# A fused attention and gated MLP kernel: four scalings and eight small copies given to GpSimd instead of ScalarE

## The chip, the cores and the metric

The kernel runs on one core of a Trainium2 chip, as one launch. The metric is the device time of that launch in microseconds (us), the median of several runs; lower is better. The core has TensorE (PE in the profile, PEld its weight loads), VectorE (DVE), ScalarE (ACT), GpSimd (POOL) and SyncE (SP), which here issues the DMAs.

## What is computed

Attention with a near window and pooled far keys, and behind it a gated MLP:

```python
# q, k, v: (4, 8, 768, 64); window 16, pooling block 32
k_sum = k.reshape(B, H, nb, block, D).max(axis=3)
v_sum = v.reshape(B, H, nb, block, D).mean(axis=3)
scores = concat([where(|i-j| < window, scale * q @ k.T, -1e9),
                 scale * q @ k_sum.T + log(block)], axis=-1)
a = exp(scores - max);  a = a / (sum(a) + 1e-9)
x = a @ concat([v, v_sum])          # -> (3072 tokens, 512)
g = x @ w_gate                      # (512, 1536)
out = (g * sigmoid(g) * (x @ w_val)) @ w_out
```

The weights arrive as 64-bit floats. The kernel turns them into float32 with integer arithmetic on DVE.

## The kernel before

The 3072 tokens are worked in 6 blocks of 512. Within a block, attention goes by 4 pairs of heads (u = 0 to 3, 128 channels each) and the MLP by 12 slices of the hidden size (j = 0 to 11). To keep precision, each MLP operand is split into a high and a low part, so that every product is three matmuls: the gate (g), the value (v) and the down projection (acc) of a slice are 12 matmuls of 128x512 each.

Two things run beside the MLP of block 0, from about 60 to 142 us. One is the attention of block 1. The other is the making of the weights: per tile `w_load` (DMA), `w_abs` (ACT, L212), `w_c1` and `w_c2` (DVE, one input, L217 and L221), `w_s1` and `w_s2` (DVE, two inputs, L229 and L236), `w_hi` (a rounding copy, mostly ACT, L187) and `w_lo` (a subtraction, DVE or POOL, L183). "gv" is a slice's gate and value weights (1024 columns), "o" its down weights (512).

The order of this stage is written out by hand in a table, PROLOGUE. Each word is a step with its arguments, and a letter behind "=" names the engine (a ScalarE, d VectorE, p GpSimd). Every engine runs its instructions strictly in the order of the table. From block 1 on, a loop sets the order.

Block 1's attention for pair u has these steps: `load`, `keys(1,u)` (pooled keys beside the near keys, POOL copies, L189), `scores` (PE, L434), `ttr0/1` (bias and row maximum, DVE, L481), `exp0/1` (ACT, L496), `rcp` (1e-9 added, reciprocal, DVE, L513 and L514), `nrm` (probabilities p times the reciprocal ri), `tr0/1` (transposes on PE, L537), `pt0/1` (copies out of PSUM, ACT), `values(1,u)` (pooled values into the rows behind the near values vw), `out` (PE, L584), `split` and `rest` (high and low part for the MLP). Block 1 spans two batch entries, so `values(1,u)` is four parts: a copy of the old pooled rows `vs` (24x512), a transpose on PE (pv, L370), a scaling of its result by 1/32 from PSUM into `vs` by ACT (L371), and a second copy. The second copy reads what L371 wrote, and L371 overwrites what the first copy read. There is one buffer of vw. The MLP's `ah` and `al` are the high and low part of the hidden activations (L187 and L183); `al(0,j)=p` is a subtraction on POOL that `down(0,j)` needs first.

The two functions that read the engine's letter (variable `on`):

```python
def a_scale(k, u):
    p, ri = U[k, u]["p"], U[k, u]["ri"]
    if on == "a":
        for i in range(2 * NTP):
            nc.scalar.mul(p[:, i, :], p[:, i, :], ri[:, i : i + 1])   # L520
        return
    (nc.vector if on == "d" else nc.gpsimd).tensor_tensor(            # L522
        out=p, in0=p, in1=ri.rearrange(...).broadcast_to([P, 2 * NTP, p.shape[2]]), op=ALU.mult)

def a_values(k, u):   # for each batch entry of the block
    nc.scalar.mul(vsum["all"][...], pv[:NB, :P], 1.0 / BLK)           # L371, if the entry begins here
    copy(on or "d", U[k, u]["vw"][KW:, i : i + n], pooled(u).broadcast_to([NB, n, P]))
```

Of the kernel before, what the change touches and what calls it, by code (L numbers as in the profile page):

```python
# [122 lines left out]
w_s1(4,gv) w_c1(3,o) w_s2(4,gv) exp1(1,0) w_hi(1,o)=a w_c2(3,o) w_lo(1,o)=d exp0(1,0) w_hi(4,gv)=a w_s1(3,o)  # L123
w_c2(2,o) w_s2(3,o) w_s1(2,o) w_load(7,gv) w_load(6,gv) rcp(1,0) down(0,1) w_lo(4,gv)=d load(1,1) silu(0,3)
w_abs(5,gv) w_hi(3,o)=a w_c1(5,gv) mul(0,3) gate(0,4) val(0,4) ah(0,2)=a w_abs(7,gv) w_c2(5,gv) w_lo(3,o)=d
w_s1(5,gv) w_s2(2,o) nrm(1,0)=a w_hi(2,o)=a w_s2(5,gv) al(0,2)=d w_hi(5,gv)=a tr0(1,0) silu(0,4) w_abs(6,gv)
w_load(4,o) tr1(1,0) pt0(1,0)=a w_abs(4,o) w_lo(2,o)=d pt1(1,0)=a down(0,2) keys(1,1) mul(0,4) w_c1(6,gv)
w_lo(5,gv)=d w_c1(4,o) scores(1,1) ah(0,4)=a w_c2(6,gv) ah(0,3)=a ttr0(1,1) exp0(1,1) ttr1(1,1) al(0,4)=d
w_load(5,o) load_values(1,0) w_load(7,o) w_load(6,o) w_c1(7,gv) w_s1(6,gv) values(1,0)=a w_load(9,gv) gate(0,5)
al(0,3)=p w_abs(5,o) w_c2(4,o) w_s2(6,gv) w_load(8,gv) w_s1(4,o) val(0,5) w_c2(7,gv) w_hi(6,gv)=a down(0,3)  # L130
out(1,0) silu(0,5) w_lo(6,gv)=d w_s2(4,o) w_c1(5,o) w_s1(7,gv) gate(0,6) w_abs(6,o) mul(0,5) w_hi(4,o)=a
w_lo(4,o)=p down(0,4) pool_values(1,1) w_s2(7,gv) w_c2(5,o) load_values(1,1) exp1(1,1) w_c1(6,o) w_s1(5,o)
w_abs(7,o) w_abs(9,gv) w_c1(9,gv) w_c1(7,o) val(0,6) w_hi(7,gv)=a w_lo(7,gv)=d w_c2(9,gv) split(1,0)=a w_s2(5,o)
rcp(1,1) silu(0,6) w_abs(8,gv) w_c2(6,o) w_s1(9,gv) load(1,2) mul(0,6) rest(1,0) w_hi(5,o)=a w_c2(7,o) ah(0,5)=a
values(1,1)=a al(0,5)=p w_load(8,o) w_load(10,gv) w_s1(6,o) gate(0,7) silu(0,7) nrm(1,1)=a w_load(9,o) val(0,7)
w_c1(8,gv) w_lo(5,o)=d w_s2(9,gv) w_hi(9,gv)=a tr0(1,1) down(0,5) mul(0,7) ah(0,7)=a pt0(1,1)=a keys(1,2)
scores(1,2) pool_values(1,2) tr1(1,1) w_lo(9,gv)=d w_s2(6,o) w_abs(8,o) w_s1(7,o) gate(0,9) ttr0(1,2) ttr1(1,2)
pt1(1,1)=a w_c2(8,gv) out(1,1) ah(0,6)=a load(1,3) w_hi(6,o)=a w_lo(6,o)=d exp0(1,2) al(0,6)=p w_s2(7,o)
w_c1(8,o) exp1(1,2) w_hi(7,o)=a w_s1(8,gv) al(0,7)=d w_s2(8,gv) w_c2(8,o) val(0,9) down(0,6) w_lo(7,o)=d
w_abs(10,gv) w_abs(9,o) w_c1(9,o) w_hi(8,gv)=a w_c1(10,gv) w_lo(8,gv)=d down(0,7) silu(0,9) rcp(1,2) w_c2(10,gv)  # L140
w_s1(10,gv) mul(0,9) split(1,1)=a w_s2(10,gv) w_c2(9,o) nrm(1,2)=a gate(0,8) tr0(1,2) w_hi(10,gv)=a keys(1,3)
w_lo(10,gv)=d w_s1(8,o) val(0,8) ah(0,9)=a rest(1,1) room(1) w_load(11,v) w_load(11,g) silu(0,8) mul(0,8)
load_values(1,2) w_load(10,o) w_load(11,o) w_s2(8,o) pt0(1,2)=a al(0,9)=p w_abs(11,v) ah(0,8)=a w_hi(8,o)=a
w_s1(9,o) al(0,8)=d w_lo(8,o)=d gate(0,10) w_c1(11,v) tr1(1,2) pt1(1,2)=a w_c2(11,v) w_s2(9,o) w_s1(11,v)
w_s2(11,v) scores(1,3) ttr0(1,3) values(1,2)=a w_hi(9,o)=a silu(0,10) down(0,8) ttr1(1,3) val(0,10) w_abs(11,g)
w_c1(11,g) w_c2(11,g) w_lo(9,o)=p out(1,2) w_s1(11,g) w_s2(11,g) w_abs(10,o) exp1(1,3) w_hi(11,g)=d w_c1(10,o)
w_hi(11,v)=a down(0,9) w_lo(11,g)=p exp0(1,3) split(1,2)=d mul(0,10) w_lo(11,v)=d w_c2(10,o) rcp(1,3) ah(0,10)=a
rest(1,2) gate(0,11) w_abs(11,o) w_c1(11,o) w_c2(11,o) load_values(1,3) nrm(1,3)=a w_s1(10,o) tr0(1,3)
pt0(1,3)=a w_s2(10,o) al(0,10)=d w_hi(10,o)=a silu(0,11) pool_values(1,3) val(0,11) tr1(1,3) pt1(1,3)=a
values(1,3)=a w_s1(11,o) w_lo(10,o)=d down(0,10) w_s2(11,o) out(1,3) w_hi(11,o)=d w_lo(11,o)=p mul(0,11)  # L150
ah(0,11)=d al(0,11)=d split(1,3)=a down(0,11) rest(1,3) load(2,0)
"""

# [730 lines left out]
```

## Time and profile before

| | |
|---|---|
| median of 3 runs (lowest to highest) | 678.55 us (678.51 to 678.67) |
| the profiled execution | 678.02 us |
| its span in the profile | 676.2 us |
| PE busy | 670.1 us (99% of the span) |
| PEld busy | 543.5 us (80%) |
| DVE busy | 331.3 us (49%) |
| ACT busy | 298.1 us (44%) |
| POOL busy | 134.4 us (20%) |

The busy shares are averages over a first part that is crowded on DVE and ACT (attention and weight making beside the MLP) and a long second part where they are half idle. What counts for a change in the first part is which engine's work PE meets late there. A busy PE is a sum of modelled durations: a stall of a few tenths between two matmuls hides in it.

### The profile page before, as it was taken

Reading aid. Unit: us, or ns where it says so; the run is one execution under the profiler, and the core shown is the slowest. Engines: PE = TensorE matmul, PEld = TensorE weight load, DVE = VectorE, ACT = ScalarE, POOL = GpSimd, SP = SyncE. Lnnn points to the kernel's source line nnn. Section 1 sums busy time; section 2 is a strip of 40 time slices with the busy share of each in tenths; the row PEclk is TensorE's granted clock in tenths of the full one; section 3 lists DMA queues with packets and bytes.
Section 4 is the critical chain, followed back from the end, with each engine's and each line's share of the span. In section 5 each row is a group of like instructions: output and inputs, shape, how many; then the busy total and the mean of one; then the engine's idle time right before and its main releaser. Section 6 shows DMA issues by size and latency. Waiting matters only on the chain.

```text
span 676.2 us, 12388 instructions
## 1 busy us (share of the span) xinstructions
PE 670.1 (99%) x4940; PEld 543.5 (80%) x4940; DVE 331.3 (49%) x919; ACT 298.1 (44%) x729; POOL 134.4 (20%) x130
## 2 busy tenths in 40 slices
PE   8999999999999999999999999999999999999997
PEld 5688888888888888888888888888888888888886
DVE  6999999946624525435346345343352451100011
ACT  6968998844441433424415424235244151211112
POOL 3110112112221212212112122121212121111110
PEclk9999999999999999999999999999999999999999
DMA  8899165145320223302404312012122000100001
GB/s 328 340 373 354 49 234 171 46 120 157 79 58 0 56 48 95 82 24 55 105 24 143 80 49 58 18 38 64 56 57 57 0 25 0 63 1 0 1 0 63
DMA packets 72058, 60.36 MB, mean 89 GB/s; under 512 B 42144, under 2 KB 60064, under 8 KB 70464
## 3 DMA queue, kind: packets, MB, share of 16 engines
q1 hardware_dynamic: 72000, 59.57, 28.6%
q8 instruction: 39, 0.64, 0.4%
q14 instruction: 19, 0.16, 0.1%
HBM read 53.26 MB, written 6.29 MB: 88 GB/s over the span
## 4 chain that ended last, share of the span: by engine, by line
PE 97%; DVE 2%; DMA 1%; issue 0%; SPq 0%; ACT 0%; DVEq 0%; ACTq 0%
PE g L619 30%; PE acc L669 29%; PE v L619 29%; PE xo L584 4%; PE sc L423 2%; DMA kq<-in_kF 1%; PE pp L537 1%; DVE p L481 1%; PE sc L434 1%; PE xo L592 1%; DVE ks L336 0%; PE pv L391 0%; PE pp L693 0%; PE pv L370 0%; DVE m_g L221 0%
## 5 line engine op out<-in xcount | busy, mean ns | idle before, releaser
L669 PE MATMUL acc<-w_o,ah 128*128 128x512 f32 x576 | 177.7, 390 | 0.0
L619 PE MATMUL g<-xh,w_gv 128*128 128x512 f32 x480 | 160.3, 395 | 0.0
L619 PE MATMUL v<-xh,w_gv 128*128 128x512 f32 x480 | 158.0, 390 | 0.0
L183 POOL TENSOR_TENSOR al<-a,ah 128x512 fp32r<-128x512 f32 x63 | 81.7, 1296 | 333.4 <-ACT ah L187 333.4
L630 DVE TENSOR_TENSOR a<-v,a 128x512 f32<-128x512 f32 x72 | 49.7, 690 | 191.6 <-PE v L619 190.8
L669 PEld LDWEIGHTS acc<-w_o,ah 128*128 128x128 f32 x576 | 108.1, 188 | 22.7
L187 ACT CAST ah<-a 128x512 fp32r<-128x512 f32 x71 | 44.0, 621 | 156.8 <-DVE a L630 156.8
L669 PE MATMUL acc<-w_o,al 128*128 128x512 f32 x288 | 113.0, 392 | 0.0
L619 PEld LDWEIGHTS g<-xh,w_gv 128*128 128x128 f32 x480 | 90.1, 188 | 21.1 <-ACT w_o L187 0.2
L619 PEld LDWEIGHTS v<-xh,w_gv 128*128 128x128 f32 x480 | 90.1, 188 | 19.1 <-issue 0.3
L625 ACT ACTIVATE a<-g 128x512 f32<-128x512 f32 x72 | 43.0, 597 | 137.9 <-PE g L619 136.3
L565 DVE STREAM_TRANSPOSE pt_short<-p_short 32x256 f32<-32x256 f32 x192 | 83.8, 436 | 25.9 <-POOL p_short L522 23.2
L619 PE MATMUL g<-xl,w_gv 128*128 128x512 f32 x240 | 93.5, 390 | 0.0
L619 PE MATMUL v<-xl,w_gv 128*128 128x512 f32 x240 | 93.4, 389 | 0.0
L669 PEld LDWEIGHTS acc<-w_o,al 128*128 128x128 f32 x288 | 54.1, 188 | 11.5 <-issue 0.2
L619 PEld LDWEIGHTS v<-xl,w_gv 128*128 128x128 f32 x240 | 45.1, 188 | 9.3
L619 PEld LDWEIGHTS g<-xl,w_gv 128*128 128x128 f32 x240 | 45.1, 188 | 8.8
L496 ACT ACTIVATE p_short<-p_short,nm 128x88 f32<-128x88 f32 x128 | 45.3, 355 | 0.2
L522 POOL TENSOR_TENSOR p_short<-p_short,ri 128x704 f32<-128x704 f32 x16 | 21.8, 1364 | 57.5 <-DVE ri L514 53.6
L619 PE MATMUL g<-xh,w_g 128*128 128x512 f32 x96 | 32.6, 400 | 0.0
L619 PE MATMUL v<-xh,w_v 128*128 128x512 f32 x96 | 31.9, 393 | 0.0
L187 ACT CAST xh<-xo 128x512 fp32r<-128x512 f32 x23 | 13.4, 591 | 38.2 <-PE xo L584 38.2
(108 smaller groups left out, 690.9 us busy)
## 6 DMA issues: line engine op xcount, KB each, us to landing
raw_gv<-in_wgv SPq DMA_DIRECT2D x10, 1024.0 KB, 11.8
raw_o<-in_wo SPq DMA_DIRECT2D x12, 512.0 KB, 7.4
out<-o SPq DMA_DIRECT2D x23, 256.0 KB, 2.0
kt<-in_kP SPq DMA_DIRECT2D x12, 384.0 KB, 4.1
vt<-in_vT SPq DMA_DIRECT2D x12, 384.0 KB, 3.9
vw<-in_vP SPq DMA_DIRECT2D x12, 384.0 KB, 3.8
kw<-in_kP SPq DMA_DIRECT2D x12, 272.0 KB, 4.7
vw<-in_vP SPq DMA_DIRECT2D x16, 192.0 KB, 3.4
```

The costliest lines, as they stand in the source:

```text
L183: (nc.vector if e == "d" else nc.gpsimd).tensor_tensor(out=out, in0=a, in1=b.bitcast(F32), op=ALU.subtract)
L187: nc.scalar.copy(out, in_)
L423: nc.tensor.matmul(sc[h][s * SQ : (s + 1) * SQ, c * SC : (c + 1) * SC], t["q"][hs, i * SQ : (i + 1) * SQ], keys[hs], start=True, stop=True,)
L434: nc.tensor.matmul(sc[h][s * QT : (s + 1) * QT, c * KC : (c + 1) * KC], t["q"][hs, qs], t["kw"][hs, i, :], start=True, stop=True,)
L496: nc.scalar.activation(out=t["p"][:, i, :kc], in_=t["p"][:, i, :kc], func=AF.Exp, scale=-1.0, bias=t["nm"][:, i : i + 1], accum_out=t["sm" ...
L522: (nc.vector if on == "d" else nc.gpsimd).tensor_tensor(out=p, in0=p, in1=ri.rearrange("p (n o) -> p n o", o=1).broadcast_to([P, 2 * NTP, ...
L565: nc.vector.transpose(out=to[r * SQ : (r + 1) * SQ, :, s * SQ : (s + 1) * SQ], in_=t["p"][s * SQ : (s + 1) * SQ, :, at : at + SQ],)
L584: nc.tensor.matmul(ps[hs, qs], vw, t["pt"][:n, h, qs], start=k not in OWN or i == 0, stop=k not in OWN)
L619: nc.tensor.matmul(ps, w[:, cs], x, start=u == 0 and n == 0, stop=u == NP - 1 and n == 2)
L625: nc.scalar.activation(out=a, in_=A.pop(("g", k, j)), func=AF.Silu)
L630: nc.vector.tensor_tensor(out=a, in0=ps, in1=a, op=ALU.mult)
L669: nc.tensor.matmul(ACC[k][i], a[:, ts], w, start=j == 0 and n == 0, stop=j == NJ - 1 and n == 2)
```

## The change

In the table, for block 1 and all four pairs, `nrm(1,u)=a` becomes `nrm(1,u)=p` and `values(1,u)=a` becomes `values(1,u)=p`. No step changes its place.

```diff
-w_s1(5,gv) w_s2(2,o) nrm(1,0)=a w_hi(2,o)=a w_s2(5,gv) al(0,2)=d w_hi(5,gv)=a tr0(1,0) silu(0,4) w_abs(6,gv)
+w_s1(5,gv) w_s2(2,o) nrm(1,0)=p w_hi(2,o)=a w_s2(5,gv) al(0,2)=d w_hi(5,gv)=a tr0(1,0) silu(0,4) w_abs(6,gv)
...
-w_load(5,o) load_values(1,0) w_load(7,o) w_load(6,o) w_c1(7,gv) w_s1(6,gv) values(1,0)=a w_load(9,gv) gate(0,5)
+w_load(5,o) load_values(1,0) w_load(7,o) w_load(6,o) w_c1(7,gv) w_s1(6,gv) values(1,0)=p w_load(9,gv) gate(0,5)
 al(0,3)=p w_abs(5,o) w_c2(4,o) w_s2(6,gv) w_load(8,gv) w_s1(4,o) val(0,5) w_c2(7,gv) w_hi(6,gv)=a down(0,3)
...
```

The same two letters change for pairs 1, 2 and 3. Each scaling, 8 instructions of 128x120 on ACT, becomes one of 128x960 on POOL.

POOL's rows from the weights of slice 3 to the keys of pair 2, before (the number behind a name's last "_" only tells buffers apart; kw_1 and vw_0 are the tiles of pairs 1 and 0, al_3 that of slice 3):

```order
L183 TENSOR_TENSOR w_gv_776<-m_gv_615,w_gv_776 128x1024
L189 COPY kw_1_876<-ks_224 128x4x24
L189 COPY kw_1_876<-ks_973 128x4x24
L183 TENSOR_TENSOR al_3_1052<-a_3_881,ah_3_1001 128x512
L183 TENSOR_TENSOR w_o_1128<-m_o_956,w_o_1128 128x512
L183 TENSOR_TENSOR al_5_1213<-a_5_1106,ah_5_1206 128x512
L189 COPY kw_2_1196<-ks_134 128x4x24
```

The same stretch with the change:

```order
L183 TENSOR_TENSOR w_gv_776<-m_gv_615,w_gv_776 128x1024
L522 TENSOR_TENSOR p_0_780<-p_0_780,ri_0_783 128x960
L189 COPY kw_1_876<-ks_224 128x4x24
L189 COPY kw_1_876<-ks_966 128x4x24
L189 COPY vw_0_1016<-vs_106 24x512 x2
L183 TENSOR_TENSOR al_3_1045<-a_3_881,ah_3_994 128x512
L183 TENSOR_TENSOR w_o_1121<-m_o_949,w_o_1121 128x512
L189 COPY vw_1_1140<-vs_106 24x512 x2
L183 TENSOR_TENSOR al_5_1206<-a_5_1099,ah_5_1199 128x512
L522 TENSOR_TENSOR p_1_996<-p_1_996,ri_1_999 128x960
L189 COPY kw_2_1189<-ks_134 128x4x24
```

Both copies of vw now stand ahead of al_3 and of al_5 on POOL, and the scaling of pair 1 stands behind al_5.

ACT's rows around the pooled values of pair 0, before:

```order
L187 CAST ah_3_1001<-a_3_881 128x512
L496 ACT_TABLE_LOAD
L496 ACTIVATE p_1_1003,sm_1_1005<-p_1_1003,nm_1_1004 128x120 x4
L187 COPY vw_0_1023<-vs_106 24x512
L371 ACTIVATE vs_106<-pv_0_1033 24x128
L187 COPY vw_0_1023<-vs_106 24x512
L212 ACTIVATE m_o_1054<-raw_o_1021 128x512
```

The same stretch with the change:

```order
L187 CAST ah_3_994<-a_3_881 128x512
L496 ACT_TABLE_LOAD
L496 ACTIVATE p_1_996,sm_1_998<-p_1_996,nm_1_997 128x120 x4
L371 ACTIVATE vs_106<-pv_0_1026 24x128
L212 ACTIVATE m_o_1047<-raw_o_1014 128x512
```

The two copies leave ACT; L371 stays there, behind the four exponentials of pair 1. The rows of PE, DVE and SP keep their order.

## Rows read from the trace of the kernel before

**Rows 1.** The page: shares of the chain that ended last, by engine.

```profile
PE 97%; DVE 2%; DMA 1%; issue 0%; SPq 0%; ACT 0%; DVEq 0%; ACTq 0%
```

**Rows 2.** Busy us (instructions) by stretch: PE, PEld, DVE, ACT, POOL; then clock, DMA, GB/s.

```profile
59.60:85.00 25.40, 25.40 (x171) 20.55 (x171) 25.38 (x50) 23.95 (x50) 2.97 (x3) 1.00 0.44 158
85.00:117.50 32.50, 32.50 (x205) 26.49 (x204) 32.01 (x62) 30.04 (x64) 6.26 (x7) 1.00 0.65 202
```

**Rows 3.** Waits, 50 to 152 us: total us, times, longest us.

```profile
DVE m_gv L217 <- ACT m_gv L212: 0.4, 1, 0.4
```

**Rows 4.** Instructions on tiles p and vw: min/median/max ns, first and last start.

```profile
L520 ACT ACTIVATE p<-p,ri x32: 379/384/407, 62.4 to 133.7; 128x120 f32<-128x120 f32 x32
L522 POOL TENSOR_TENSOR p<-p,ri x3: 1790/1791/1847, 11.8 to 17.9; 128x960 f32<-128x960 f32 x3
...
L187 ACT COPY vw<-vs x8: 614/618/619, 74.8 to 139.5; 24x512 f32<-24x512 f32 x8
```

**Rows 5.** Groups by form, POOL's copies of 384 elements: busy us, mean ns.

```profile
L189 POOL COPY kw<-ks 128x384 f32<-128x384 f32 x12 | 6.6, 553 | 18.5 <-PE sc L423 18.5
```

**Rows 6.** Timeline of POOL and DVE: start us, us, operation; pairs that meet.

```profile
14.51 1.85 POOL L522 TENSOR_TENSOR p<-p,ri 128x960 f32<-128x960 f32 x1 [0.88 <-DVE ri L514]
15.49 1.15 DVE L221 TENSOR_SCALAR m_g<-m_g 128x512 int32<-128x512 int32 x1
...
16.68 0.70 DVE L229 SCALAR_TENSOR_TENSOR m_g<-raw_g,m_g 128x512 int32<-128x512 int32 x1
...
17.87 1.79 POOL L522 TENSOR_TENSOR p<-p,ri 128x960 f32<-128x960 f32 x1 [1.51 <-DVE ri L514]
19.22 0.99 DVE L236 SCALAR_TENSOR_TENSOR m_g<-raw_g,m_g 128x512 int32<-128x512 int32 x1
...
83.93 0.41 DVE L221 TENSOR_SCALAR m_o<-m_o 128x512 int32<-128x512 int32 x1
...
115.10 1.22 DVE L183 TENSOR_TENSOR w_gv<-m_gv,w_gv 128x1024 fp32r<-128x1024 f32 x1
115.19 1.26 POOL L189 COPY kw<-ks 128x96 f32<-128x96 f32 x1 [12.50 <-DVE ks L336]
```

**Rows 7.** Timeline of DVE and PE around the scaling of pair 0.

```profile
59.66 1.17 DVE L183 TENSOR_TENSOR w_gv<-m_gv,w_gv 128x1024 fp32r<-128x1024 f32 x1
60.76 0.69 DVE L217 TENSOR_SCALAR m_gv<-m_gv 128x1024 f32<-128x1024 f32 x1
...
66.64 0.68 DVE L183 TENSOR_TENSOR w_o<-m_o,w_o 128x512 fp32r<-128x512 f32 x1
...
67.63 0.63 PE L669 MATMUL acc<-w_o,ah 128*128 128x512 f32 x2
```

**Rows 8.** Timeline of POOL, ACT and PE around the copies of pair 0.

```profile
71.43 1.29 POOL L183 TENSOR_TENSOR al<-a,ah 128x512 fp32r<-128x512 f32 x1 [2.92 <-ACT ah L187]
...
75.43 0.27 ACT L371 ACTIVATE vs<-pv 24x128 f32<-24x128 f32 x1
...
76.82 0.39 PE L669 MATMUL acc<-w_o,al 128*128 128x512 f32 x1
```

**Rows 9.** Timeline of ACT, DVE and PE around pair 1.

```profile
91.70 0.26 ACT L371 ACTIVATE vs<-pv 24x128 f32<-24x128 f32 x1
...
92.60 0.74 DVE L229 SCALAR_TENSOR_TENSOR m_o<-raw_o,m_o 128x512 int32<-128x512 int32 x1
...
94.58 0.60 PE L537 MATMUL pp<-consts,p 128*120 128x128 f32 x4
...
97.93 1.21 DVE L183 TENSOR_TENSOR w_gv<-m_gv,w_gv 128x1024 fp32r<-128x1024 f32 x1
...
99.24 0.48 PE L619 MATMUL g<-xh,w_gv 128*128 128x512 f32 x1
```

**Rows 10.** Timeline of DVE and PE around the scaling of pair 2.

```profile
110.97 1.23 DVE L229 SCALAR_TENSOR_TENSOR m_gv<-raw_gv,m_gv 128x1024 int32<-128x1024 int32 x1
...
117.45 0.39 PE L619 MATMUL g<-xh,w_gv 128*128 128x512 f32 x1
```

More of the change, by code (lines that the diff above doesn't have):

```diff
@@ L134 @@
 rcp(1,1) silu(0,6) w_abs(8,gv) w_c2(6,o) w_s1(9,gv) load(1,2) mul(0,6) rest(1,0) w_hi(5,o)=a w_c2(7,o) ah(0,5)=a
-values(1,1)=a al(0,5)=p w_load(8,o) w_load(10,gv) w_s1(6,o) gate(0,7) silu(0,7) nrm(1,1)=a w_load(9,o) val(0,7)
+values(1,1)=p al(0,5)=p w_load(8,o) w_load(10,gv) w_s1(6,o) gate(0,7) silu(0,7) nrm(1,1)=p w_load(9,o) val(0,7)
 w_c1(8,gv) w_lo(5,o)=d w_s2(9,gv) w_hi(9,gv)=a tr0(1,1) down(0,5) mul(0,7) ah(0,7)=a pt0(1,1)=a keys(1,2)
@@ L140 @@
 w_abs(10,gv) w_abs(9,o) w_c1(9,o) w_hi(8,gv)=a w_c1(10,gv) w_lo(8,gv)=d down(0,7) silu(0,9) rcp(1,2) w_c2(10,gv)
-w_s1(10,gv) mul(0,9) split(1,1)=a w_s2(10,gv) w_c2(9,o) nrm(1,2)=a gate(0,8) tr0(1,2) w_hi(10,gv)=a keys(1,3)
+w_s1(10,gv) mul(0,9) split(1,1)=a w_s2(10,gv) w_c2(9,o) nrm(1,2)=p gate(0,8) tr0(1,2) w_hi(10,gv)=a keys(1,3)
 w_lo(10,gv)=d w_s1(8,o) val(0,8) ah(0,9)=a rest(1,1) room(1) w_load(11,v) w_load(11,g) silu(0,8) mul(0,8)
@@ L144 @@
 w_s1(9,o) al(0,8)=d w_lo(8,o)=d gate(0,10) w_c1(11,v) tr1(1,2) pt1(1,2)=a w_c2(11,v) w_s2(9,o) w_s1(11,v)
-w_s2(11,v) scores(1,3) ttr0(1,3) values(1,2)=a w_hi(9,o)=a silu(0,10) down(0,8) ttr1(1,3) val(0,10) w_abs(11,g)
+w_s2(11,v) scores(1,3) ttr0(1,3) values(1,2)=p w_hi(9,o)=a silu(0,10) down(0,8) ttr1(1,3) val(0,10) w_abs(11,g)
 w_c1(11,g) w_c2(11,g) w_lo(9,o)=p out(1,2) w_s1(11,g) w_s2(11,g) w_abs(10,o) exp1(1,3) w_hi(11,g)=d w_c1(10,o)
 w_hi(11,v)=a down(0,9) w_lo(11,g)=p exp0(1,3) split(1,2)=d mul(0,10) w_lo(11,v)=d w_c2(10,o) rcp(1,3) ah(0,10)=a
-rest(1,2) gate(0,11) w_abs(11,o) w_c1(11,o) w_c2(11,o) load_values(1,3) nrm(1,3)=a w_s1(10,o) tr0(1,3)
+rest(1,2) gate(0,11) w_abs(11,o) w_c1(11,o) w_c2(11,o) load_values(1,3) nrm(1,3)=p w_s1(10,o) tr0(1,3)
 pt0(1,3)=a w_s2(10,o) al(0,10)=d w_hi(10,o)=a silu(0,11) pool_values(1,3) val(0,11) tr1(1,3) pt1(1,3)=a
-values(1,3)=a w_s1(11,o) w_lo(10,o)=d down(0,10) w_s2(11,o) out(1,3) w_hi(11,o)=d w_lo(11,o)=p mul(0,11)
+values(1,3)=p w_s1(11,o) w_lo(10,o)=d down(0,10) w_s2(11,o) out(1,3) w_hi(11,o)=d w_lo(11,o)=p mul(0,11)
 ah(0,11)=d al(0,11)=d split(1,3)=a down(0,11) rest(1,3) load(2,0)
```

## The prediction

> **What bounds the kernel now.** I read the chain that ended last first. PE holds 97% of it [rows 1], so time changes only where PE starts something later or earlier. The table of busy time by stretch comes next: from 59.6 to 117.5 us PE has no idle time, at a granted clock of 1.00, and DVE is busy 57.4 of 57.9 us, ACT 54.0, POOL only 9.2 [rows 2]. So POOL has room, ACT little and DVE none. In this stretch a wait put upon DVE is not made good; it is handed on, step by step, to the next weight or activation that PE needs. The list of waits then says what ACT costs: DVE waited for it once, 0.4 us [rows 3]. A lighter ACT can hardly shorten anything: PE waits for nobody that ACT feeds.
>
> **What the change removes and adds.** Off ACT go 32 scalings of 0.384 us (12.3 us of busy time) and 8 copies of 0.618 us (4.9 us) [rows 4]. Onto POOL come 4 scalings of 1.79 us [rows 4] and 8 copies. POOL has no row of a 24x512 copy; its 384-element copy took 0.553 us on average [rows 5], so I take 0.6, with 0 and 1.3 as bounds (wholly covered; held up as long as the copy in [rows 6]). As lengths alone this would be harmless: the scaling is one instruction instead of eight.
>
> **What POOL and DVE do to each other** decides. In the timelines, instructions of the two that read or write SBUF alone do not overlap; the one that starts second waits for the whole of the other. A one-input DVE step of 512 columns takes 0.41 us alone; started inside a POOL scaling it took 1.15, ending 0.28 us after the scaling. A two-input step takes 0.70 alone and 0.99 when started 0.44 us before the end of another scaling. The other way, a 96-element POOL copy that started just after a DVE subtraction took 1.26 us, more than twice the mean of one four times as large [rows 5, 6]. DVE steps that read PSUM, and reductions, ran beside POOL undisturbed. Behind each reciprocal DVE goes straight on with weight work, so each POOL scaling now falls among steps that it excludes. The sum goes by place; "late" is against the times of before, separately for DVE and PE.
>
> *Pair 0, scaling.* The reciprocal is done at 59.7 us, when DVE has begun a subtraction that lasts to 60.83; POOL gets its turn there and holds it until 62.6. DVE's next step, due at 60.76 [rows 7], loses 1.7 us: DVE is 1.7 late (bounds 0 and 1.8). The low part of slice 2's down weights then ends at 66.64 + 0.68 + 1.7 = 69.0, and PE's second matmul of that down projection, at 67.63 [rows 7], waits for it: **PE 1.4 late**.
>
> *Pair 0, copies.* The first copy costs DVE 0.2. On POOL the subtraction for `al(0,3)` now queues behind the second copy, which waits for L371 on ACT, which stands behind four exponentials, which wait for DVE's maxima. Before, POOL had done it at 71.43, long ahead of PE's use at 76.82. Now L371 starts at 75.43 - 0.62 (first copy gone) + 1.9 = 76.7 and ends at 77.0; 0.3 until DVE lets go and 0.6 for the copy give 77.9; a DVE step that waited goes first, 0.3; the subtraction, 1.29, ends at 79.5. PE wants it at 76.82 + 1.4 = 78.2 [rows 8]: **PE 2.7 late**. DVE waits for that copy (0.5) and subtraction (1.2), which had cost it nothing as it ran beside the maxima, and is 3.6 late (bounds 1.9 and 4.5).
>
> *Pair 1.* L371 starts at 91.70 - 0.62 + 3.6 = 94.7 and ends at 95.0; then follow on POOL the copy to 95.6, `al(0,5)` to 96.9, a waiting DVE step to 97.2, and the scaling to 99.0. PE wants the scaled p for its transposes at 94.58 + 2.7 = 97.3: PE 4.4 late. DVE loses 0.6 more than before beside `al(0,5)`, 1.6 at the step of 92.60 beside the scaling, and 0.2 beside copies: 6.0 late. The low part of slice 9's gate weights ended 0.1 us before PE took it, at 97.93 + 1.21 against 99.24 [rows 9]. It now ends at 105.1, so that **PE is 6.0 late**, whatever the transposes did.
>
> *Pair 2.* The step of 110.97 waits 1.6 for the scaling: DVE 7.6 late. Slice 10's gate weights end at 115.10 + 1.22 + 7.6 = 123.9; PE wants them at 117.45 + 6.0 = 123.5 [rows 6, 10]: **PE 6.5 late**.
>
> *Pair 2's copies and pair 3.* Here no row gives a price at PE. The bounds are 0 (the lateness of DVE that PE has not yet met is worked off by the waits that DVE has for PE) and 1.6 (one more scaling met in full). I take 0, since the weight making runs out there.
>
> After the stage PE is the bound to the end, so nothing is won back. The sum is +6.5 us on the profiled execution's 678.02, so 684.5. The median lies 0.5 us above that execution, so the forecast is 685.0 us. The 0.4 us that DVE may win from ACT [rows 3] is left out. SP issues the same DMAs in the same order; POOL issues none.
>
> **The rivals.** *ACT was in the way and POOL harms nobody.* Were POOL's spans only unlucky neighbours of DVE's long ones, ACT would be 17 us lighter, DVE would win its 0.4 us, and POOL's order alone would cost nothing, since everything on ACT and DVE comes earlier: 678.2 us, not slower. It decides if DVE's steps beside a scaling keep the lengths they have alone. The pairs of [rows 6] speak against it; for it speaks that POOL has much room. Chance 0.10, of which 0.02 goes to a gain over 0.2%.
>
> *Only one-input steps are excluded.* Then the first scaling starts at once, and DVE loses 0.8 there, 0.7 at the copies and 0.6 beside `al(0,5)`; the steps of 92.60 and 110.97, which have two inputs, lose nothing. With POOL's queue that gives PE about 2.5 us: 681.0 us. Against it stand the two-input step stretched to 0.99 and the subtraction that held a copy [rows 6]. Half the meetings missed would give nearly the same (3.2 us). Chance 0.14. The Trainium skill, Advanced Engine Details and Errata, section VectorE Performance Modes (Mode Summary), names only the two-port modes as what blocks GpSimd, by which the time would be this rival's. Its page SBUF — State Buffer, section Who interferes with whom, counts instructions with two SBUF inputs too and lets the loser wait for the whole instruction, by which it would be my 685.0; the trace agrees with the second (0.70 against 0.99 us).
>
> *The meetings pile up.* If POOL must also wait for a full DVE step at two more of its turns (1.2 us each, [rows 6]) and pair 3 costs its 1.6, PE is 10.5 late: 689.0 us. Chance 0.10. For it: the chain of pair 1 has POOL, ACT and DVE each waiting for one another.
>
> **How the numbers follow.** The main case has 0.66; its own range is 682 to 688, by half the meetings and by the 1.6 of pair 3 with one more full wait. Taking in the second rival and half of the last makes 680.5 to 688.5; left out is the first rival, 0.10, and part of the last. A measurement of this kernel tells about 0.2%, 1.4 us, from no change. Slower by more has 0.66 + 0.14 + 0.10 = 0.90; within it 0.08; faster 0.02.
>
> **What would show it.** In the changed profile the one-input step behind the first reciprocal should last some 2.4 us instead of 0.69, and the steps at 92.60 and 110.97 (then some 4 to 6 us later) about 1.6 us more. PE should list waits at a down projection for POOL's `al` and DVE's low parts, 1 to 2 us each, all before 125 us; behind 150 us every row should only be shifted. It is wrong if DVE's steps keep their lengths, if PE shows no waits, or if PE's lateness shrinks again after 142 us.

## The result, and the profile after

The changed kernel takes **686.62 us** (median of 4 runs, 686.32 to 686.71) against 678.61 us (4 runs): the ratio is 1.0116, with a 95% interval of 1.0101 to 1.0132, so 8.0 us slower (6.9 to 9.0). The forecast was 685.0 us in a range of 680.5 to 688.5. The profiled execution took 686.70 us with a span of 684.9.

From the page of the changed kernel, the engines' busy time and, below it, the chain that ended last:

```profile
PE 672.7 (98%) x4940; PEld 542.7 (79%) x4940; DVE 341.2 (50%) x919; ACT 284.0 (41%) x689; POOL 150.6 (22%) x142
...
PE 82%; DVE 12%; ACT 2%; DMA 1%; issue 1%; SPq 0%; ACTq 0%; DVEq 0%
```

DVE runs the same 919 instructions as before and is busy 9.9 us longer (341.2 against 331.3 us): a step that is held shows as a longer step, not as idle time. POOL is busy 16.2 us longer (134.4 before), although its new work, at the lengths that it has alone (a copy of 24x512 that met nothing took 0.62 us), is 4 x 1.79 + 8 x 0.62 = 12.1 us. ACT lost 14.1 us. DVE now holds 12% of the chain, where it had 2% [rows 1].

The table by stretch of the changed kernel (columns as in [rows 2], the stretches a little longer because everything is later):

```profile
59.60:85.00 25.40, 23.58 (x159) 18.27 (x158) 25.34 (x46) 17.06 (x31) 6.47 (x7) 1.00 0.36 129
85.00:123.50 38.50, 36.59 (x217) 28.75 (x216) 38.34 (x66) 26.74 (x55) 12.47 (x11) 1.00 0.61 191
123.50:150.00 26.50, 25.29 (x195) 19.70 (x194) 25.88 (x55) 15.49 (x38) 12.11 (x12) 1.00 0.12 36
```

PE was busy without a gap to 117.5 us [rows 2]; now it lacks 1.8, 1.9 and 1.2 us, 4.9 in all. The rest of its lateness (below) hides in longer matmuls: PE is busy 2.6 us longer for the same 4940. DVE is as full as before, ACT is not: 17.1 of 25.4 us, where it had 24.0. What ACT gained is waiting. In its list of waits one group grew from 2.5 us in the kernel before to:

```profile
ACT w_gv L187 <- DVE m_gv L236: 13.4, 5, 4.9
```

PE's list of waits in the changed kernel (total us, times, longest us; the waits in the start-up left out):

```profile
PE acc L669 <- DVE al L183: 1.0, 2, 0.9
PE pp L537 <- POOL p L522: 1.0, 1, 1.0
PE acc L669 <- POOL al L183: 0.9, 1, 0.9
PE acc L669 <- DVE w_o L183: 0.9, 2, 0.5
PE g L619 <- DVE w_gv L183: 0.5, 2, 0.3
PE g L619 <- ACT a L625: 0.4, 1, 0.4
PE v L619 <- ACT a L625: 0.2, 1, 0.2
```

None of these seven was in the list before. Three name work of DVE, two work of POOL, and two work of ACT, which itself waits for DVE's weights. The timeline of POOL and DVE shows what lies behind them:

```profile
60.26 2.59 POOL L522 TENSOR_TENSOR p<-p,ri 128x960 f32<-128x960 f32 x1 [8.75 <-DVE ri L514]
61.12 2.28 DVE L217 TENSOR_SCALAR m_gv<-m_gv 128x1024 f32<-128x1024 f32 x1
...
78.29 1.32 POOL L183 TENSOR_TENSOR al<-a,ah 128x512 fp32r<-128x512 f32 x1
78.41 2.28 DVE L236 SCALAR_TENSOR_TENSOR m_gv<-raw_gv,m_gv 128x1024 int32<-128x1024 int32 x1
...
95.80 1.39 POOL L183 TENSOR_TENSOR al<-a,ah 128x512 fp32r<-128x512 f32 x1
95.96 1.78 DVE L229 SCALAR_TENSOR_TENSOR m_o<-raw_o,m_o 128x512 int32<-128x512 int32 x1
97.15 2.24 POOL L522 TENSOR_TENSOR p<-p,ri 128x960 f32<-128x960 f32 x1
97.66 2.27 DVE L217 TENSOR_SCALAR m_gv<-m_gv 128x1024 f32<-128x1024 f32 x1
...
116.54 2.04 POOL L522 TENSOR_TENSOR p<-p,ri 128x960 f32<-128x960 f32 x1 [8.99 <-DVE ri L514]
116.96 2.69 DVE L229 SCALAR_TENSOR_TENSOR m_gv<-raw_gv,m_gv 128x1024 int32<-128x1024 int32 x1
```

Each pair meets as in [rows 6]. The one-input step behind the first reciprocal lasts 2.28 us, where it took 0.69 [rows 7]. POOL had waited for the subtraction in front of it (2.59 us for an instruction of 1.79). Slice 3's subtraction on POOL, 7 us later than before [rows 8], holds a step of 1.22 us until it lasts 2.28. At pair 1 `al(0,5)` and the scaling hold two steps one behind the other. At 116.96 a two-input step of 1.23 us [rows 10] lasts 2.69.

And PE, at the places of [rows 7 to 10] and at two later ones:

```profile
69.34 0.73 PE L669 MATMUL acc<-w_o,ah 128*128 128x512 f32 x2
...
79.67 0.50 PE L669 MATMUL acc<-w_o,al 128*128 128x512 f32 x1 [0.89 <-POOL al L183]
...
99.44 0.65 PE L537 MATMUL pp<-consts,p 128*120 128x128 f32 x4 [0.95 <-POOL p L522]
...
105.25 0.50 PE L619 MATMUL g<-xh,w_gv 128*128 128x512 f32 x1 [0.23 <-DVE w_gv L183]
...
123.93 0.47 PE L619 MATMUL g<-xh,w_gv 128*128 128x512 f32 x1 [0.29 <-DVE w_gv L183]
...
131.54 0.50 PE L619 MATMUL v<-xh,w_gv 128*128 128x512 f32 x1 [0.24 <-ACT a L625]
...
145.94 0.74 PE L669 MATMUL acc<-w_o,ah 128*128 128x512 f32 x2 [0.54 <-DVE w_o L183]
```

In this execution the first load of keys came late (PE's wait for it is 1.8 us, 0.6 before), and everything from 25 to 60 us lies 0.4 us behind before. With that taken off, PE is late at these seven places by 1.3, 2.5, 4.5, 5.6, 6.1, 6.6 and 7.4 us. From 150 to 200 us every row is shifted by the same 7.8 us. From there to 600 us the shift creeps up by another 0.5 us: a value matmul that started at 600.05 us before now starts at 608.71. I do not count this to the change, because the same creep is in the trace of the order alone, an experiment below without any new work on POOL (0.3 us late at 160 us, 0.7 at 600), and is not in that of the scalings only (3.9 and 3.7).

### The profile page after: what moved, and what is told of

The parts are those of the page before. It is cut to its first block, busy times and chain, and to the rows that moved or that the text cites. A ratio compares the mean times of both kernels' runs of the same rounds, so it can differ in the third digit from the quotient of the medians.

```text
span 684.9 us, 12369 instructions
## 1 busy us (share of the span) xinstructions
PE 672.7 (98%) x4940; PEld 542.7 (79%) x4940; DVE 341.2 (50%) x919; ACT 284.0 (41%) x689; POOL 150.6 (22%) x142
## 4 chain that ended last, share of the span: by engine, by line
PE 82%; DVE 12%; ACT 2%; DMA 1%; issue 1%; SPq 0%; ACTq 0%; DVEq 0%
PE g L619 26%; PE v L619 25%; PE acc L669 25%; PE xo L584 3%; PE sc L423 2%; DVE p L481 1%; DVE m_gv L236 1%; DVE w_gv L183 1%; DVE m_o L229 1%; DMA kq<-in_kF 1%; DVE m_o L236 1%; DVE m_gv L229 1%; DVE m_gv L217 1%; ACT p L496 1%; DVE w_o L183 1%
## 5 line engine op out<-in xcount | busy, mean ns | idle before, releaser
L565 DVE STREAM_TRANSPOSE pt_short<-p_short 32x256 f32<-32x256 f32 x192 | 83.8, 436 | 25.9 <-POOL p_short L522 23.2
L669 PEld LDWEIGHTS acc<-w_o,al 128*128 128x128 f32 x288 | 54.1, 188 | 14.1 <-POOL al L183 1.3
```

The costliest lines, as they stand in the source:

```text
L565: nc.vector.transpose(out=to[r * SQ : (r + 1) * SQ, :, s * SQ : (s + 1) * SQ], in_=t["p"][s * SQ : (s + 1) * SQ, :, at : at + SQ],)
L669: nc.tensor.matmul(ACC[k][i], a[:, ts], w, start=j == 0 and n == 0, stop=j == NJ - 1 and n == 2)
```

## The experiments

The theory: a POOL instruction that reads SBUF and a DVE step that touches SBUF alone exclude each other, and DVE, which has no spare time here, hands the lost time to PE (exclusion). The rivals: PE is late only because results come late or in another order on POOL's queue (queue order); only one-input steps of DVE are excluded. Each kernel was timed beside the kernel before on the same chip, whose median was 678.2 to 678.7 us.

| kernel | median us | over before, us | ratio (95% interval) |
|---|---|---|---|
| the change | 686.62 | 8.0 | 1.0116 (1.0101 to 1.0132) |
| scalings only | 682.51 | 3.8 | 1.0051 (1.0036 to 1.0066) |
| copies only | 681.81 | 3.1 | 1.0041 (1.0026 to 1.0056) |
| idle product | 682.33 | 3.6 | 1.0051 (1.0036 to 1.0066) |
| idle fill | 679.15 | 0.4 | 1.0005 (0.9995 to 1.0014) |
| scalings on DVE | 681.66 | 3.5 | 1.0052 (1.0037 to 1.0067) |
| subtractions first | 685.03 | 6.9 | 1.0102 (1.0087 to 1.0118) |
| pair 1's scaling | 679.61 | 1.4 | 1.0023 (1.0014 to 1.0033) |
| pair 1's scaling, first cover | 680.64 | 2.5 | 1.0039 (1.0024 to 1.0054) |
| pairs 2 and 3 | 680.69 | 2.0 | 1.0030 (1.0019 to 1.0042) |
| pair 1's scaling, second cover | 679.02 | 0.3 | 1.0005 (0.9996 to 1.0015) |
| its order alone | 679.14 | 0.5 | 1.0007 (0.9998 to 1.0017) |

### The two halves of the change

The scalings only, in all four pairs:

```diff
-nrm(1,u)=a
+nrm(1,u)=p
```

> Only the four scalings go to GpSimd; the copies stay on ScalarE. Exclusion (a GpSimd instruction and a VectorE step that touches SBUF alone do not overlap; the later one waits): VectorE loses 1.2 to 1.7 us at each scaling, and TensorE ends 4 to 5.5 us later than before, with the step behind the first reciprocal at some 2.3 us. Queue order alone (TensorE is late only where a GpSimd result comes late): every scaled p is there before its transposes except perhaps pair 1's, so 0 to 0.5 us. Only one-input steps excluded: about 1.5 us.

Measured: 3.8 us over before, just under the range of exclusion and far over the two others. In its trace PE is late by 1.3 us at slice 2's down projection, 3.1 at slice 9's gate and 3.9 at the end, always behind a weight or an `al` that DVE makes; no wait for a scaled p is in its list.

The copies only:

```diff
-values(1,u)=a
+values(1,u)=p
```

> Only the eight copies go to GpSimd; the scalings stay on ScalarE. Exclusion with queue order: the subtraction for slice 3's hidden part comes behind the second copy and L371, about 1 us too late for its down projection, and then stands beside excluded VectorE steps; in all 2 to 3.5 us. Queue order alone: 1 us. If the sum is additive, this and the scalings alone make up the 8.0 us of the whole change.

Measured: 3.1 us over before. The timeline of POOL and DVE around slice 3's subtraction:

```profile
75.04 0.89 POOL L189 COPY vw<-vs 24x512 f32<-24x512 f32 x1 [6.16 <-ACT vs L371]
76.01 1.33 POOL L183 TENSOR_TENSOR al<-a,ah 128x512 fp32r<-128x512 f32 x1
76.14 2.29 DVE L236 SCALAR_TENSOR_TENSOR m_gv<-raw_gv,m_gv 128x1024 int32<-128x1024 int32 x1
```

The subtraction comes 0.9 us too late for its down projection, as queue order has it, and while it runs it holds a DVE step of 1.22 us until 2.29, as exclusion has it. Both parts are there. The halves sum to 6.9 us, the whole change costs 8.0; the difference lies within the intervals.

### GpSimd work that nobody waits for

On the kernel before, with scalings and copies on ScalarE:

```diff
-nrm(1,u)=a
+nrm(1,u)=a idle(1,u)
...
+    def a_idle(k, u):
+        t["pt"] = two.tile([KC, 2, TOK], F32, tag="pt", ...)   # filled only later, by pt0 and pt1
+        r = ri.broadcast_to([KC, 2 * NTP, KC])
+        nc.gpsimd.tensor_tensor(out=z, in0=r, in1=r, op=ALU.mult)   # z: 960 columns of pt
```

> The kernel before (scalings and copies on ScalarE) plus, behind each reciprocal of block 1, one GpSimd product of the same length (120x960) that reads the reciprocals and writes a buffer that is dead at that time; nothing needs its result but the later copy into the same buffer, microseconds afterwards. Exclusion: VectorE is held as by the real scalings, and TensorE ends 4 to 5.5 us later, as with the scalings alone. Queue order or late results alone: 0 to 0.3 us, since nobody waits for it.

Measured: 3.6 us over before, as much as the real scalings cost (3.8), with the same lateness at the same places. The pair at the first reciprocal:

```profile
59.96 2.66 POOL L535 TENSOR_TENSOR pt<-ri 120x960 f32<-120x960 f32 x1 [8.72 <-DVE ri L514]
60.89 2.28 DVE L217 TENSOR_SCALAR m_gv<-m_gv 128x1024 f32<-128x1024 f32 x1
```

DVE's step is held to the same 2.28 us. No result of POOL is late here (PE's list has no wait for POOL), and ACT has all of its old work; queue order alone cannot make this. It also shows that ACT's relief was worth nothing that can be measured.

The same with fills in place of the product:

```diff
-        r = ri.broadcast_to([KC, 2 * NTP, KC])
-        nc.gpsimd.tensor_tensor(out=z, in0=r, in1=r, op=ALU.mult)
+        nc.gpsimd.tensor_copy(z[:, :, :1], ri)
+        for _ in range(2):
+            nc.gpsimd.memset(z, 0.0)
```

> As the idle product, but GpSimd only writes: a copy of 8 elements and two fills of 120x960, together some 2 us. If a fill excludes every VectorE step that touches SBUF alone, 4 to 6 us as with the product. If a fill excludes only one-input steps (they need the shared way to write), the two-input steps beside the fills of pairs 1 and 2 keep their 0.7 and 1.2 us, and the cost is 1 to 3 us. If it excludes none, under 0.3 us.

Measured: 0.4 us, within the noise (in its trace PE is 0.6 late), below what I gave for either kind of exclusion. The fills are as long as a scaling, 1.86 us for the two when undisturbed:

```profile
111.66 1.23 DVE L229 SCALAR_TENSOR_TENSOR m_gv<-raw_gv,m_gv 128x1024 int32<-128x1024 int32 x1
111.74 1.86 POOL L536 MEMSET pt<- 120x960 f32 x2
...
132.43 2.02 POOL L536 MEMSET pt<- 120x960 f32 x2 [0.18 <-POOL pt L534]
133.64 1.09 DVE L221 TENSOR_SCALAR m_o<-m_o 128x512 int32<-128x512 int32 x1
```

The two-input step at 111.66 keeps its 1.23 us beside a fill; beside the scaling it lasted 2.69. The one-input step at 133.64 took 0.43 us before; here it ends 0.28 us after the second fill, just as one ended behind a scaling in [rows 6]. So it is at the other places: the two-input steps beside a fill keep their lengths, and the four one-input steps that met one last 0.2 to 0.7 us longer. A fill holds one-input steps until it ends and two-input steps not at all; a product holds both. DVE is busy 1.2 us longer than before with the fills and 5.4 us longer with the product. For two-input steps, then, it is not the time that POOL is busy that costs, but that its instruction reads. How much of the low cost is due to this, and how much to the few one-input steps that stood beside the fills, the run does not separate. The Trainium skill, SBUF — State Buffer, section Who interferes with whom, says that a DVE instruction with two SBUF inputs contends with a GpSimd instruction that reads SBUF, not with one that only writes; the trace agrees with both halves (2.69 and 1.23 us).

### The scalings on DVE

```diff
-nrm(1,u)=a
+nrm(1,u)=d
```

> The four scalings on VectorE itself (1.15 us each in the prologue's row), copies on ScalarE. Exclusion: VectorE loses 1.15 us per pair, a little less than it loses while GpSimd does them (1.2 to 1.7), so 2.5 to 4.5 us and not more than the scalings on GpSimd alone. If GpSimd does relieve VectorE of anything, this must be the slowest of all, over 5 us.

Measured: 3.5 us over before. The instruction takes 1.15 us on DVE. Giving the scalings to POOL (3.8) costs this kernel what it costs to give them to DVE itself, within the intervals.

### The order on POOL's queue

```diff
-... values(1,0)=p w_load(9,gv) gate(0,5)
-al(0,3)=p w_abs(5,o) ...
+... al(0,3)=p values(1,0)=p w_load(9,gv) gate(0,5)
+w_abs(5,o) ...
-values(1,1)=p al(0,5)=p ...
+al(0,5)=p values(1,1)=p ...
```

> The whole change, but the subtractions of slices 3 and 5 stand ahead of the copies of pairs 0 and 1 on GpSimd. Exclusion with queue order: slice 3's subtraction falls beside the row maxima again and costs nothing; the wait at its down projection (1.4 us) goes, and 1 to 2.5 us of the 8.0 come back: 5.5 to 7 us over before. Exclusion alone, without any part of the queue: 8 us stay.

Measured: 6.9 us over before, at the upper end of the range; 1.1 us less than the change. PE's wait for slice 3's subtraction is gone. At pair 1's transposes the swap did less, since the scaling stands behind both copies and the subtraction in either order: PE waits 1.7 us for the scaled p, where it waited 1.0. At slice 9's gate PE is 4.6 us late, where it was 5.6.

### One scaling, held and covered

Only pair 1's scaling on GpSimd, where the change has it:

```diff
-... silu(0,7) nrm(1,1)=a w_load(9,o) val(0,7)
+... silu(0,7) nrm(1,1)=p w_load(9,o) val(0,7)
```

> Only pair 1's scaling goes to GpSimd, behind slice 5's subtraction as in the change. Exclusion: VectorE loses 1.5 to 2.7 us at the steps of 92.6 and 93.3 us, which slice 9's gate weights (0.1 us of slack) hand on to TensorE: 1.3 to 2.5 us slower. Queue order alone: the scaled p comes at about the time of the transposes, 0 to 0.3 us.

Measured: 1.4 us over before. PE waits for no result of POOL there. One DVE step carries nearly all of it (alone it takes 0.7 us):

```profile
92.41 1.97 POOL L522 TENSOR_TENSOR p<-p,ri 128x960 f32<-128x960 f32 x1
92.65 2.27 DVE L229 SCALAR_TENSOR_TENSOR m_o<-raw_o,m_o 128x512 int32<-128x512 int32 x1
```

The first try to cover it:

```diff
-... w_s2(5,o)
-rcp(1,1) silu(0,6) w_abs(8,gv) w_c2(6,o) w_s1(9,gv) load(1,2) mul(0,6) rest(1,0) w_hi(5,o)=a ...
-values(1,1)=a al(0,5)=p ... silu(0,7) nrm(1,1)=a ... pt0(1,1)=a keys(1,2)
+... w_s2(5,o) load(1,2)
+rcp(1,1) nrm(1,1)=p silu(0,6) w_abs(8,gv) keys(1,2) mul(0,6) rest(1,0) w_c2(6,o) w_s1(9,gv) w_hi(5,o)=a ...
+values(1,1)=a al(0,5)=p ... silu(0,7) ... pt0(1,1)=a
```

> As the last, but the scaling stands first behind the reciprocal on GpSimd, and VectorE's reduction of pair 2's keys, its product with the value matmul (from PSUM) and the low part of pair 0 (from PSUM) stand beside it, 2.3 us of steps that GpSimd did not disturb. Exclusion: the scaling now costs VectorE nothing; what is left is that slice 5's subtraction meets excluded steps, 0 to 1.2 us. If a GpSimd instruction hurts whatever stands beside it, as slow as the last one.

A miss: 2.5 us over before, more than uncovered. The trace says why:

```profile
89.54 1.79 POOL L522 TENSOR_TENSOR p<-p,ri 128x960 f32<-128x960 f32 x1 [6.95 <-DVE ri L514]
91.28 0.26 POOL L189 COPY kw<-ks 128x96 f32<-128x96 f32 x1
91.58 0.95 DVE L336 TENSOR_REDUCE ks<-kt 128x24 f32<-128x768 f32 x1 [2.17 <-POOL kw L189]
```

The scaling took its undisturbed 1.79 us, but the reduction that was to stand beside it did not start. `keys(1,2)` begins with a POOL copy of the old pooled keys, queued behind the scaling, and the reduction overwrites what that copy reads. DVE stood idle for 2.2 us. The wait was of my own making and says nothing of exclusion.

The second try takes that copy ahead of the scaling (step `ka`) and adds the other reduction:

```diff
-... w_s2(5,o)
-rcp(1,1) silu(0,6) w_abs(8,gv) w_c2(6,o) w_s1(9,gv) load(1,2) mul(0,6) rest(1,0) w_hi(5,o)=a w_c2(7,o) ah(0,5)=a
-values(1,1)=a al(0,5)=p w_load(8,o) ... silu(0,7) nrm(1,1)=a w_load(9,o) val(0,7)
-w_c1(8,gv) w_lo(5,o)=d w_s2(9,gv) w_hi(9,gv)=a ... keys(1,2)
-scores(1,2) pool_values(1,2) tr1(1,1) ...
+... w_s2(5,o) load(1,2)
+ka(1,2) rcp(1,1) nrm(1,1)=p silu(0,6) w_abs(8,gv) mul(0,6) rest(1,0) w_hi(5,o)=a ah(0,5)=a
+values(1,1)=a pool_values(1,2) al(0,5)=p kb(1,2) w_lo(5,o)=d w_s1(9,gv) w_s2(9,gv) w_c2(6,o) w_c2(7,o) w_load(8,o) ... silu(0,7) w_load(9,o) val(0,7)
+w_c1(8,gv) w_hi(9,gv)=a ...
+scores(1,2) tr1(1,1) ...
```

> Pair 1's scaling alone on GpSimd, now with 3.2 us of VectorE steps beside it and beside slice 5's subtraction that GpSimd did not disturb (product and low part from PSUM, two reductions), and without the wait that the first try made: there the reduction of the keys had to wait for a GpSimd copy queued behind the scaling. Exclusion: scaling and subtraction cost VectorE nothing, 0 to 0.4 us over before, against 1.4 for the same scaling where it stood. If GpSimd work hurts whatever stands beside it, 1.2 us or more.

And its control, the same order with the scaling back on ScalarE:

```diff
-ka(1,2) rcp(1,1) nrm(1,1)=p silu(0,6) ...
-... silu(0,7) w_load(9,o) val(0,7)
+ka(1,2) rcp(1,1) silu(0,6) ...
+... silu(0,7) nrm(1,1)=a w_load(9,o) val(0,7)
```

> The new order of VectorE's steps alone, pair 1's scaling on ScalarE at its old place: the control for the run before. The number and length of VectorE's steps are the same and slice 9's gate weights are due at the same time, so within 0.4 us of before by every theory.

Measured: 0.3 and 0.5 us over before, both within the noise of before and of each other. DVE and POOL in the second try:

```profile
89.50 0.67 DVE L630 TENSOR_TENSOR a<-v,a 128x512 f32<-128x512 f32 x1
89.73 1.79 POOL L522 TENSOR_TENSOR p<-p,ri 128x960 f32<-128x960 f32 x1 [6.73 <-DVE ri L514]
90.09 0.68 DVE L183 TENSOR_TENSOR xl<-xo,xh 128x512 fp32r<-128x512 f32 x1
90.69 0.94 DVE L355 TENSOR_REDUCE vr<-vt 128x24 f32<-128x768 f32 x1
91.48 1.29 POOL L183 TENSOR_TENSOR al<-a,ah 128x512 fp32r<-128x512 f32 x1
91.54 0.94 DVE L336 TENSOR_REDUCE ks<-kt 128x24 f32<-128x768 f32 x1
92.40 0.92 DVE L183 TENSOR_TENSOR w_o<-m_o,w_o 128x512 fp32r<-128x512 f32 x1
```

The scaling (89.73 to 91.52) and slice 5's subtraction (91.48 to 92.77) lie beside four steps that either read PSUM or are reductions, and all of them keep the lengths that they have alone. Only the fifth, a two-input step, meets the end of the subtraction and lasts 0.92 us instead of 0.68. The same scaling costs 1.4 us beside the wrong steps and nothing measurable beside these.

### Pairs 2 and 3 alone

```diff
-nrm(1,2)=a ... values(1,2)=a ... nrm(1,3)=a ... values(1,3)=a
+nrm(1,2)=p ... values(1,2)=p ... nrm(1,3)=p ... values(1,3)=p
```

> Scalings and copies of pairs 2 and 3 alone on GpSimd. The trace of the change has TensorE 1.7 us later from pair 2's copies to the end of the stage, where the prediction took 0. Exclusion: pair 2's scaling costs 0.4 after 1.1 of slack, the rest up to 1.7: 1 to 2.5 us. If that late part was only a leftover of the lateness of pairs 0 and 1: under 0.6 us.

Measured: 2.0 us over before. PE's rows at four places, the first three of them the places of the last three rows shown of the change:

```profile
117.94 0.47 PE L619 MATMUL g<-xh,w_gv 128*128 128x512 f32 x1 [0.26 <-DVE w_gv L183]
...
125.56 0.50 PE L619 MATMUL v<-xh,w_gv 128*128 128x512 f32 x1 [0.25 <-ACT a L625]
...
139.96 0.74 PE L669 MATMUL acc<-w_o,ah 128*128 128x512 f32 x2 [0.49 <-DVE w_o L183]
...
144.05 0.50 PE L669 MATMUL acc<-w_o,al 128*128 128x512 f32 x1 [0.18 <-DVE al L183]
```

Before, these four started at 117.45 [rows 10] and, the fourth at 141.81:

```profile
124.55 0.39 PE L619 MATMUL v<-xh,w_gv 128*128 128x512 f32 x1
...
138.12 0.63 PE L669 MATMUL acc<-w_o,ah 128*128 128x512 f32 x2
```

So PE is late by 0.5 behind pair 2's scaling and by 1.0, 1.8 and 2.2 us from then on: 1.7 us come behind slice 10's gate, with pairs 0 and 1 untouched.

## Why the prediction was right, and where it was off

- **The bound.** PE bound the stage, DVE had no time to spare and ACT's relief shortened nothing: shown by the idle product, which leaves ACT all its work and costs the same as the scalings. One size was misread, without weight in the sum: the records of the 32 scalings overlap on ACT and fill 9.6 us of it, not 12.3, so that ACT was relieved of 14.1 us and not of 17.
- **What POOL and DVE do to each other.** Shown: idle product (nobody waits, 3.6 us), covered scaling (0.3 us), uncovered one (1.4 us). The rival in which only one-input steps are excluded falls by the two-input step of 2.69 us. It would have given 681.0. The Trainium skill, Advanced Engine Details and Errata, section VectorE Performance Modes (Mode Summary), names only the two-port modes, which speaks for that rival; this trace does not bear it out (2.69 us against 1.23). The rule as I had put it, for all steps that read or write SBUF alone, was too wide in turn: beside a fill, which reads nothing, a two-input step kept its 1.23 us.
- **Pair 0, scaling.** Predicted: step 1.7 us longer, PE 1.4 late. Measured 1.6 and 1.3.
- **Pair 0, copies.** Predicted PE 2.7 late, measured 2.5, by the chain that was named: L371 on ACT, second copy, subtraction, down projection. DVE's two losses were forecast as 0.5 and 1.2; they were 0.4 and 1.1.
- **Pair 1.** Predicted PE 4.4 late at the transposes and 6.0 at slice 9's gate, measured 4.5 and 5.6. The steps that were held lay one place further down the order than forecast: `al(0,5)` held the two-input step and the scaling the one behind it, with nearly the same sum.
- **Pair 2, scaling.** Predicted 6.5, measured 6.1.
- **Pair 2's copies and pair 3: the term that was mis-sized.** I took 0 between bounds of 0 and 1.6 and gave as the reason that the weight making runs out there. The change shows 1.7 us (6.1 to 7.8), and pairs 2 and 3 alone show 1.7 behind slice 10's gate too. The weight making does not run out before 142 us: DVE is busy 25.9 of the last 26.5 us in the stretch from 123.5. The lateness that DVE carried was met by slice 10's value matmul (through ACT, which itself waits for DVE), by its down weights and by the last `al`. Nor was DVE's lateness worked off by its waits for PE; it grew on (the 0.4 us of the late start taken off) from 7.1 us at slice 10's gate weights (122.56 against 115.10) to 8.8 at its down weights (145.20 against 135.99). In the trace of the change, pair 2's two copies held a two-input step each, for 0.4 us, and pair 3's scaling held a step of 0.43 us for 1.1:

```profile
139.07 1.79 POOL L522 TENSOR_TENSOR p<-p,ri 128x960 f32<-128x960 f32 x1 [1.63 <-ACT ah L187]
139.57 1.57 DVE L217 TENSOR_SCALAR m_o<-m_o 128x512 f32<-128x512 f32 x1
```

Here the upper bound was the better value: with it the forecast would have been 686.6. That this comes so near to the 686.62 measured is partly luck, since pairs 0 to 2 cost 0.4 us less than forecast (6.1 for 6.5).

- **The signs.** The steps grew nearly as foretold: the one behind the first reciprocal to 2.28 us (some 2.4 foretold), the other two by 1.0 and 1.5 us (about 1.6). PE's waits did not come as foretold: they are 0.2 to 1.0 us each and not 1 to 2, and three of them come after 125 us, behind the term above.
- **After the stage** nothing was won back: the shift stays at 7.8 us to 200 us, as forecast, and does not shrink after that.

What stays open: whether a version with all four scalings covered would match the kernel before was not tried. It could hardly beat it, since PE has no idle time there to win.

## What to carry to other kernels

A half-idle GpSimd is not free room beside a full VectorE. Before an elementwise step goes there, look in the timeline at which VectorE steps will stand beside it: those that read PSUM and the reductions here ran undisturbed, those between SBUF tiles were held until a GpSimd product ended. Move the step and its cover together, and check what else is queued behind it on GpSimd: here a subtraction stood behind a copy that waits for another engine, and its matmul waited.

## What the hardware showed that I had not expected

GpSimd's fills, which read nothing, took as long as a scaling (1.86 us) and cost 0.4 us where the product cost 3.6; a two-input VectorE step beside them kept its 1.23 us, while a one-input step of 0.43 us was held to the end of a fill and lasted 1.09. And when both engines always had a next instruction, neither kept the other out for long: whichever waited went next, so that at pair 1 two VectorE steps in a row were held by two GpSimd instructions in a row (1.78 and 2.27 us for steps of 0.7).
